# Weight conversions cast two steps behind their values, low parts on VectorE, and an opening in another order

## The chip, the cores and the metric

The kernel runs on one core of a Trainium2 chip. The metric is the device time of one launch in microseconds (us), the median of three runs. The core's engines work beside each other, each through its own queue in order: TensorE (PE: matmuls and transposes; weight loads are listed as PEld), VectorE (DVE), ScalarE (ACT), GpSimd (POOL) and SyncE (SP, which here only issues DMAs). Semaphores make one engine wait for another.

## What is computed

The reference chains three layers for 4 sequences of 576 tokens with 512 channels:

```python
attn = softmax(mask128(q @ k.T / 8 - slope * distance))      # 8 heads of 64, window of 128
x    = (attn @ v) laid out as tokens x 512
u    = x + real(fft(fft(x, axis=1), axis=2))                 # mixing
un   = (u - mean) / sqrt(var + 1e-6)
x2   = u + relu(un @ w_ch1) @ w_ch2                          # 2048 hidden; w_ch1, w_ch2 are float64
e    = argmax(x2 @ w_gate), or the expert of the token before it (local gate)
out  = p[e] * (relu(x2 @ w1[e]) @ w2[e])                     # 8 experts, 1024 hidden
```

## The kernel before

All large products run in fp32r as three matmuls on a high and a low part of each operand (`mm3`, L176 to L178); the high part is a cast (`split`, L172, ACT), the low part the rest after it (L173).

**Opening** (`opening`, written out by hand: inside `manual_schedule` the instructions of PE, DVE, ACT and POOL keep the program's order). Attention of sequence 0 runs over ten units; a unit is 128 query rows (or 65) for four heads. Its steps: `scores` on PE, bias and maximum on DVE (L395 to L398); `exps` on ACT (L405) with a small POOL addition (L406); `flip`: four PE transposes (L414), an ACT copy `w` (L418), POOL selects on `w` (L419, L421); `values` on PE (L433); `natural`: PE transposes back (L453) and a division on DVE (L461). Unit u's scores stand beside the flip of u-2, the values of u-3 and the natural of u-4. Then come the folds of x (L521 to L533), the first Fourier products `zps` (L950), their copies to SBUF (L988, `low_row` L581 and L582), the second products `pc` (L567), which `spread` adds to x (L559, L560), the statistics (L757), the normalised rows `u` (L791, L793), their transposes and the first MLP matmuls. POOL casts a small table `alt` (L859) that has come by DMA.

**Weights.** w_ch1 and w_ch2 arrive as 64-bit words in blocks of 128 x 512. Turning a block to fp32 takes a scaling on ACT (`early64`, L248, or L284) and a shift of the lower word (L250 on ACT for the first half of the weights, L285 on DVE for the second), then two DVE operations (`values32`, L286, L287), then `split`: cast on ACT, low part on POOL. A chunk of 256 hidden units has four blocks, two for its `t1` and two for its `t2`. In `load_weights64` both values of a pair come first, then both casts, then both low parts.

**Lanes.** After the opening a planner (`run`) interleaves generators by due times: MLP pieces, conversions, attention and mixing of the next sequence. `late_` and `behind` keep instructions behind others on their engine; Tile's own scheduler then settles the order on each engine. The MLP runs over nine groups of 256 tokens twice, first with 1024 hidden units (chunks A), then with the other 1024 (chunks B). Chunk 0 of A is converted in the opening, chunks 1 to 3 beside the first MLP group (`conversions`), chunks B later (`second`).

**Routing.** In the second MLP pass `finish_group` of the group before is stepped once per MLP piece: transposes, `route` (gate products, copy `lt` L1153, transposes `pn` L1157, softmax and argmax), then for some groups `assign` (scans over the tokens, `rows` L1219, `place` L1225). The experts follow.

Of the kernel before, what the change touches and what calls it, by code (L numbers as in the profile page):

```python
# [10 lines left out]
F32 = mybir.dt.float32  # L11
F32R = mybir.dt.float32r
# [41 lines left out]
MIX = ((25.1, 10), (51.1, 11), (77.1, 12), (102.1, 9))  # L54
CONV_ = (25, 9.5)
CONV2 = (8, 38)
# [108 lines left out]
def build(ctx, tc, a, out):  # L165
# [86 lines left out]

    def load_weights64(chunks, i, c, wp, words, early=None):
        q = CB // 2
        for _ in early or ():
            pass
        ms = []
        for j in range(2):
            ms.append(values32(raws[c][j], words, early is not None))
            if j == 0:  # L260
                yield
        t1 = wp.tile([P, 2, 4, CB], F32R, tag="w1", name="t1")
        for j in range(2):
            split(t1[:, 0, :, j * q:(j + 1) * q], t1[:, 1, :, j * q:(j + 1) * q], ms[j], nc.gpsimd)
        chunks[i] = (t1, None)
        yield
        ms = []
        for j in range(2):
            ms.append(values32(raws[c][2 + j], words, early is not None))
            if j == 0:  # L270
                yield
        t2 = wp.tile([P, 2, CB // P, DM], F32R, tag="w2", name="t2")
        for j in range(2):
            split(t2[:, 0, j].rearrange("p (k f) -> p k f", k=4), t2[:, 1, j].rearrange("p (k f) -> p k f", k=4), ms[j], nc.gpsimd)
        chunks[i] = (t1, t2)
        yield

    def values32(r, words, small=False):
# [4 lines left out]
        if not small:  # L283
            nc.scalar.activation(y.bitcast(F32), y.bitcast(F32), AF.Copy, scale=BIAS)  # L284
            nc.vector.tensor_single_scalar(wl, wl, 29, op=ALU.logical_shift_right)  # L285
# [79 lines left out]
    def attention(b, between=None):  # L365

        xs = xss[b] = [slab([P, 2, DM], F32, "x", "x", XB) for _ in range(3)]
        units = [(g, i) for g in range(2) for i in range(5)]
        copy = nc.vector.tensor_copy if b == 0 else nc.scalar.copy
# [98 lines left out]
        for u in range(len(units) + VL + 1):  # L468
            if ahead < 4 and u in (0, 2, 5):
                g, p = parts[ahead]  # L470
                R[g, p] = load_part(b, g, p)
                ahead += 1
            if u < len(units):
                scores(u)
            if 1 <= u < len(units) + 1:
                exps(u - 1)
            yield

            def fill():
                if b == 0 and u >= len(units) - 1:  # L480
                    spin(SPIN_)

            def back():
                if VL < u:
                    natural(u - VL - 1)

            def weights():
                if FL <= u < len(units) + FL:
                    flip(u - FL)
# [12 lines left out]
            yield  # L502
# [10 lines left out]
    def fold(xs, kt, eng=nc.vector, xf=None):  # L513
# [5 lines left out]
        if kt == 0:  # L519

            nc.vector.scalar_tensor_tensor(out=xe, in0=xb, scalar=inner[:, 0:1], in1=xa, op0=ALU.mult, op1=ALU.add)  # L521
        else:
            nc.vector.tensor_tensor(out=xe[0:m], in0=xa[0:m], in1=xb[0:m], op=ALU.add)
        if kt == 2:
            nc.scalar.copy(xe[32:33], xa[32:33])
        nc.vector.tensor_tensor(out=xe[0:n, 1:HN], in0=xe[0:n, 1:HN], in1=xe[0:n, DM - 1:HN:-1], op=ALU.add)
# [219 lines left out]
    def normalise(gs, xT, j, src=None):  # L746
# [106 lines left out]
    def tables():  # L853

        with tc.issue_after(last["load"].ins):
            alt32 = slab([P, KE], F32, "alt32", "m", MB)
            for t, x in ((alt32, "alt"), (tab1, "tab1"), (tab2, "tab2")):
                nc.sync.dma_start(out=t, in_=a[x])
        nc.gpsimd.tensor_copy(alt, alt32)  # L859

# [11 lines left out]
    def conversions():  # L872
        def places():
            for i in range(2 * (FA // CB - 1)):
                if i % 3:
# [3 lines left out]
                else:  # L879
                    yield sm.tile([P, 2 * CB], U32, tag="t64", name="t64", bufs=2)  # L880
                    yield sm.tile([P, 2 * CB], U32, tag="t64", name="t64", bufs=2)

        place = places()
        for c in range(1, FA // CB):
            yield from load_weights64(chunksA, c, c, wpA, lambda: next(place), soon64[c])

# [37 lines left out]
    def opening():  # L924
# [56 lines left out]

        idle[0] = ps_g.tile([P, DM], F32, tag="g", name="idle")
        bank.update({(1, 0): a2[:, 1], (1, 1): ps_h1.tile([P, DM], F32, tag="h", name="zps")})
        Z = [slab([P, 2, K1], F32, f"z{cs}", "m", MB) for cs in range(2)]
# [19 lines left out]
        def value():  # L1004
            ms.append(values32(raws[0][len(ms)], lambda: next(place), True))

# [17 lines left out]
        nrm = prepare(0, (xs[0][:, 0], xs[1][:, 0]))  # L1024
        words.step(4)
        for _ in range(3):
            next(nrm)
        next(nrm)
        value()
# [21 lines left out]
    def late_(it):  # L1051

        while True:
# [4 lines left out]
            if r is END:  # L1058
                return
            yield r  # L1060

    lanes = [lane(SETUP, 8, 1, setup()), lane(CONV_[0], CONV_[1], 4 * (FA // CB - 1), late_(conv)),
             lane(MLP_[0], MLP_[1], 4 * FA // CB * 9, mlp_first())]
# [18 lines left out]
    def second():  # L1082

        words = lact.tile([P, 4, 2 * CB], U32, tag="xTe", name="t64", bufs=1)
        turns = iter(range(4 * nB))
        for c in range(nB):
            it = load_weights64(chunksB, c, nA + c, wpB, lambda: words[:, next(turns) % 4])
            while True:
                with behind():
                    if next(it, END) is END:  # L1090
                        break
                yield

# [7 lines left out]
    now = min(x[0] for x in lanes)  # L1101
    lanes.append(lane(now + CONV2[0], CONV2[1], 4 * nB, second()))
    run(lanes)
# [38 lines left out]

    def route(gs, xT, apart):
        n = len(gs) * P
# [50 lines left out]
    def assign(b, half=None):  # L1195
# [26 lines left out]
        def place(g, st_, m):  # L1222
# [12 lines left out]
            if b == B - 1 and g in TAIL:  # L1235
                for x in placed:
                    tc.declare_no_dep(w.ins, x, reason="each token has a slot of its own")
                placed.append(w.ins)

        ready = None  # L1240
        for t in ts:
# [223 lines left out]
    def finish_group(gs, x2s, j):  # L1465
# [5 lines left out]
        if apart:  # L1471
            yield
        yield from route(gs, x2T, apart)
        if j in after:
# [193 lines left out]
```

## Time and profile before

| | us |
|---|---|
| median of three runs | 934.81 (934.53 to 934.94) |
| the profiled execution | 935.08 |
| its span | 933.4 |
| PE busy | 886.8 |
| DVE busy | 520.9 |
| ACT busy | 378.8 |
| POOL busy | 251.4 |

Busy time is the union of an engine's instructions. The views differ: the slices (windows) give busy time and granted clock of a stretch; the waits give an engine's idle time with what ended it; the timeline gives single instructions, with the idle time ahead of one in brackets and the releaser behind the arrow.

### The profile page before, as it was taken

Reading aid. Unit: us, or ns where it says so; the run is one execution under the profiler, and the core shown is the slowest. Engines: PE = TensorE matmul, PEld = TensorE weight load, DVE = VectorE, ACT = ScalarE, POOL = GpSimd, SP = SyncE. Lnnn points to the kernel's source line nnn. Section 1 sums busy time; section 2 is a strip of 40 time slices with the busy share of each in tenths; the row PEclk is TensorE's granted clock in tenths of the full one; section 3 lists DMA queues with packets and bytes.
Section 4 is the critical chain, followed back from the end, with each engine's and each line's share of the span. In section 5 each row is a group of like instructions: output and inputs, shape, how many; then the busy total and the mean of one; then the engine's idle time right before and its main releaser. Section 6 shows DMA issues by size and latency. Waiting matters only on the chain.

```text
span 933.4 us, 16250 instructions
## 1 busy us (share of the span) xinstructions
PE 886.8 (95%) x5954; PEld 747.2 (80%) x5958; DVE 520.9 (56%) x1326; ACT 378.8 (41%) x1003; POOL 251.4 (27%) x374
## 2 busy tenths in 40 slices
PE   8986899999999998999999999999999999999993
PEld 4665677777787897899888888887888898888882
DVE  4879957746746577521333635456874665556410
ACT  4684563653553245421121111113544554445410
POOL 2425731350322046210111222223331221032100
PEclk8998999999999999999999999999999999999997
DMA  9933251451403593263444252545635765555100
GB/s 321 333 124 103 84 188 59 145 161 44 137 25 102 158 359 111 68 158 69 113 113 104 51 117 70 114 113 189 188 118 183 239 221 172 173 181 177 68 21 20
DMA packets 103361, 128.20 MB, mean 137 GB/s; under 512 B 10577, under 2 KB 72401, under 8 KB 103239
## 3 DMA queue, kind: packets, MB, share of 16 engines
q1 hardware_dynamic: 77958, 102.98, 33.7%
q0 software_dynamic: 22720, 19.36, 9.5%
q10 hardware_dynamic: 2592, 4.72, 1.4%
q8 instruction: 49, 0.80, 0.4%
q14 instruction: 42, 0.34, 0.1%
HBM read 98.68 MB, written 30.19 MB: 138 GB/s over the span
## 4 chain that ended last, share of the span: by engine, by line
PE 70%; DVE 14%; issue 6%; ACT 3%; DMA 3%; POOL 2%; SPq 0%; DVEq 0%; POOLq 0%; ACTq 0%
PE hps L176 9%; PE acc L176 9%; PE hps L178 9%; PE hps L177 9%; PE acc L177 8%; PE acc L178 8%; PE s L393 3%; PE o L433 3%; DVE t L286 3%; PE tps L641 2%; PE zps L615 2%; DVE t L287 2%; PE acc L688 2%; PE pt L414 1%; PE xps L453 1%
## 5 line engine op out<-in xcount | busy, mean ns | idle before, releaser
L669 ACT ACTIVATE h<-hps 128x256 fp32r<-128x256 f32 x152 | 58.2, 383 | 264.5 <-PE hps L178 264.1
L672 DVE SCALAR_TENSOR_TENSOR h<-hps,h 128x256 fp32r<-128x256 f32 x152 | 63.8, 420 | 150.3 <-ACT h L669 149.5
L176 PE MATMUL acc<-t,h 128*128 128x512 f32 x312 | 129.2, 414 | 2.7 <-ACT t L172 2.5
L177 PE MATMUL acc<-t,h 128*128 128x512 f32 x312 | 124.1, 398 | 1.7 <-POOL t L173 1.7
L178 PE MATMUL acc<-t,h 128*128 128x512 f32 x312 | 123.4, 396 | 0.2 <-DVE h L672 0.2
L173 DVE TENSOR_TENSOR t<-we,t 128x512 fp32r<-128x512 f32 x128 | 85.9, 698 | 35.1 <-ACT t L172 34.4
L172 ACT CAST t<-we 128x512 fp32r<-128x512 f32 x128 | 74.6, 618 | 29.7 <-PE acc L688 17.2
L176 PE MATMUL hps<-xT,t 128*128 128x256 f32 x288 | 84.5, 294 | 1.4 <-DVE h L672 1.3
L176 PE MATMUL hps<-xTb,t 128*128 128x256 f32 x288 | 84.1, 292 | 0.0
L176 PE MATMUL hps<-xTe,t 128*128 128x256 f32 (+6 forms) x288 | 83.5, 290 | 0.0
L177 PE MATMUL hps<-xTe,t 128*128 128x256 f32 (+6 forms) x288 | 83.0, 288 | 0.0
L177 PE MATMUL hps<-xT,t 128*128 128x256 f32 x288 | 82.3, 286 | 0.6 <-DVE xT L173 0.6
L178 PE MATMUL hps<-xTe,t 128*128 128x256 f32 (+6 forms) x288 | 82.9, 288 | 0.0
L178 PE MATMUL hps<-xT,t 128*128 128x256 f32 x288 | 82.2, 286 | 0.6 <-POOL t L173 0.6
L178 PE MATMUL hps<-xTb,t 128*128 128x256 f32 x288 | 81.5, 283 | 0.0
L177 PE MATMUL hps<-xTb,t 128*128 128x256 f32 x288 | 81.5, 283 | 0.0
L405 ACT ACTIVATE t<-t,mx 128x128 f32<-128x128 f32 (+1 forms) x160 | 62.6, 393 | 40.6 <-DVE mx L398 35.5
L178 PEld LDWEIGHTS acc<-t,h 128*128 128x128 f32 x312 | 58.6, 188 | 15.0 <-DVE h L672 1.2
L176 PEld LDWEIGHTS acc<-t,h 128*128 128x128 f32 x312 | 58.9, 189 | 14.7 <-issue 3.1
L177 PEld LDWEIGHTS acc<-t,h 128*128 128x128 f32 x312 | 59.1, 189 | 9.6 <-POOL t L173 2.3
L672 DVE SCALAR_TENSOR_TENSOR hE<-hps,hE 128x256 fp32r<-128x256 f32 (+3 forms) x96 | 29.7, 338 | 60.5 <-ACT hE L669 60.2
L176 PEld LDWEIGHTS hps<-xT,t 128*128 128x128 f32 x288 | 55.1, 192 | 7.8 <-DVE h L672 1.9
(311 smaller groups left out, 2047.2 us busy)
## 6 DMA issues: line engine op xcount, KB each, us to landing
we<-in_w SPq DMA_DIRECT2D x64, 512.0 KB, 4.4
rw<-in_w_ch SPq DMA_DIRECT2D x32, 512.0 KB, 8.9
qkt<-in_qk SPq DMA_DIRECT2D x15, 642.0 KB, 4.2
nd<-xT SPq DMA_DIRECT2D x18, 512.0 KB, 3.7
xTb<-nd POOLq DMA_DIRECT2D x18, 512.0 KB, 6.0
vt<-in_v SPq DMA_DIRECT2D x16, 384.0 KB, 10.4
pd<-y ACTq DMA_DIRECT2D x18, 256.0 KB, 3.2
ub<-ud SPq DMA_DIRECT2D x18, 256.0 KB, 2.8
```

What stands on the lines that cost most here:

```text
L172: last["hi"] = nc.scalar.copy(hi, src)
L173: return (eng or nc.vector).tensor_tensor(out=lo, in0=src, in1=hi.bitcast(F32), op=ALU.subtract)
L176: nc.tensor.matmul(o, lhsT=wh, rhs=xh, start=start, stop=False, **kw)
L177: nc.tensor.matmul(o, lhsT=wh, rhs=xl, start=False, stop=False, **kw)
L178: return nc.tensor.matmul(o, lhsT=wl, rhs=xh, start=False, stop=stop, **kw)
L286: nc.vector.scalar_tensor_tensor(out=t, in0=y, scalar=3, in1=wl, op0=ALU.logical_shift_left, op1=ALU.bitwise_or)
L287: nc.vector.scalar_tensor_tensor(out=t, in0=y, scalar=0x80000000, in1=t, op0=ALU.bitwise_and, op1=ALU.bitwise_or)
L393: nc.tensor.matmul(o[h], lhsT=qt[r, x, q0:q0 + m], rhs=qt[r, x, k0:k0 + n0 + n1], start=i > 0, stop=True)
L405: nc.scalar.activation(t[0:m, j], t[0:m, j], AF.Exp, bias=mx[0:m, j:j + 1], scale=-1.0, accum_out=sums[0:m, j:j + 1])
L433: nc.tensor.matmul(o[h * D:(h + 1) * D, x, 0:m], lhsT=v[:, OWN[i] - z, (2 * x + h) * D:(2 * x + h + 1) * D], rhs=w[:, z, 2 * h + x, 0:m], ...
L669: last["relu"] = nc.scalar.activation(h[:, 0:n], hps[:, 0:n], AF.Relu)
L672: last["rest"] = nc.vector.scalar_tensor_tensor(out=h[:, lo:lo + c1 - c0], in0=hps[:, c0:c1], scalar=0.0, in1=h[:, c0:c1].bitcast(F32), op ...
```

## The change

1. Conversions (`convert` takes the place of `load_weights64`) go block by block. Step b makes the values of block b, the cast and the low part of block b-2, and the scaling of block b+1. The low part is a DVE subtraction (it was POOL's). For 12 blocks there are 14 steps (12 before) in a lane of 11 units (9.5 before); for chunks B there are 18 steps (16) in the same 38 units. What is left of `early64` is issued two instructions per block, behind the last MLP instructions.
2. The opening: `flip(0)` of sequence 0 comes ahead of `exps(1)`; the cast of `alt` comes nine steps later; the third fold no longer copies one row on ACT, since POOL zeroes that row of x at the start of each attention; the products of `zps` lie in other PSUM tiles; the statistics of the first half come ahead of the second half's products.
3. Three routing steps are set apart by one MLP piece each: `pn` of the eighth group, and the first `rows` of `assign` for sequences 0 and 1.

```diff
-CONV_ = (25, 9.5)
+CONV_ = (25, 11)
...
+    def convert(chunks, wp, cs, base, words, early=None):
+        blocks = [(c, h, j) for c in cs for h in range(2) for j in range(2)]
+        n, q = len(blocks), CB // 2
+        ts, made = {}, {}
+
+        def lift(b):
+            c, h, j = blocks[b]
+            if early is None:
+                lifted(raws[base + c][2 * h + j])
+                return
+            with behind() if "ffn" in last else nullcontext():
+                for _ in range(2):
+                    next(early[c], None)
+
+        lift(0)
+        for b in range(n + 2):
+            if b >= 2:
+                c, h, j = blocks[b - 2]
+                if j == 0:
+                    made[h] = wp.tile([P, 2, 4, CB] if h == 0 else [P, 2, CB // P, DM], F32R, tag=f"w{h + 1}", name=f"t{h + 1}")
...
+                t = ts.pop(b - 2)
+                nc.scalar.copy(hi, t)
+            if b < n:
+                ts[b] = values32(raws[base + blocks[b][0]][2 * blocks[b][1] + blocks[b][2]], words)
+            if b >= 2:
+                nc.vector.tensor_tensor(out=lo, in0=t, in1=hi.bitcast(F32), op=ALU.subtract)
+                if j == 1:
+                    chunks[c] = (made[0], made[1] if h else None)
+            if b + 1 < n:
+                lift(b + 1)
+            yield
...
     def attention(b, between=None):
 
         xs = xss[b] = [slab([P, 2, DM], F32, "x", "x", XB) for _ in range(3)]
+        nc.gpsimd.memset(xs[2][32:33, 1], 0.0)
...
+            if b == 0 and u == FL:
+                flip(0)
             if 1 <= u < len(units) + 1:
                 exps(u - 1)
...
-            nc.vector.tensor_tensor(out=xe[0:m], in0=xa[0:m], in1=xb[0:m], op=ALU.add)
-        if kt == 2:
-            nc.scalar.copy(xe[32:33], xa[32:33])
+            nc.vector.tensor_tensor(out=xe[0:n], in0=xa[0:n], in1=xb[0:n], op=ALU.add)
...
             nc.vector.bn_stats(st[:, i], src[i])
+            if i + 1 < n and not later:
+                yield
...
-                tables()
+                alt32 = tables()
+            if n == 13:
+                nc.gpsimd.tensor_copy(alt, alt32)
...
-                a2 = ps_a.tile([P, 2, DM], F32, tag="acc", name="zps")
-                bank.update({(0, 0): s2[:, 1], (0, 1): a2[:, 0], (0, 2): s2[:, 0]})
+                bank.update({(0, 0): s2[:, 1], (0, 1): ps_h1.tile([P, DM], F32, tag="h", name="zps"), (0, 2): s2[:, 0]})
...
-        bank.update({(1, 0): a2[:, 1], (1, 1): ps_h1.tile([P, DM], F32, tag="h", name="zps")})
+        a2 = ps_a.tile([P, 2, DM], F32, tag="acc", name="zps")
+        bank.update({(1, 0): a2[:, 0], (1, 1): a2[:, 1]})
...
         next(kb0)
+        nrm = prepare(0, (xs[0][:, 0], xs[1][:, 0]))
+        next(nrm)
+        next(nrm)
...
         nc.scalar.copy(lt[:, 0:n], ps[0:r2, 0:n])
         yield
+        if late_copy:
+            yield
...
+        if half is None and b < 2:
+            yield
         ready = None
         for t in ts:
             new = rows(t)
```

## Rows read from the trace of the kernel before

**Rows 1.** The page: engines over the span, and two-input subtractions on VectorE.

```profile
PE 886.8 (95%) x5954; PEld 747.2 (80%) x5958; DVE 520.9 (56%) x1326; ACT 378.8 (41%) x1003; POOL 251.4 (27%) x374
...
L173 DVE TENSOR_TENSOR t<-we,t 128x512 fp32r<-128x512 f32 x128 | 85.9, 698 | 35.1 <-ACT t L172 34.4
```

**Rows 2.** Windows: length, then busy of PE, PEld, DVE, ACT, POOL; clock, DMA, GB/s.

```profile
0.00:25.00 25.00, 21.12 (x132) 12.25 (x132) 11.81 (x23) 10.95 (x45) 5.11 (x17) 0.86 0.87 309
...
50.00:75.00 25.00, 21.53 (x131) 15.92 (x132) 20.23 (x45) 19.32 (x40) 7.35 (x7) 1.00 0.30 104
75.00:100.00 25.00, 18.79 (x119) 13.91 (x117) 25.00 (x37) 12.16 (x40) 15.52 (x14) 0.86 0.17 53
100.00:125.00 25.00, 20.38 (x166) 15.50 (x165) 19.53 (x37) 13.95 (x51) 16.42 (x29) 1.00 0.52 154
125.00:150.00 25.00, 24.98 (x213) 20.02 (x212) 10.66 (x27) 11.83 (x42) 6.52 (x13) 1.00 0.40 128
...
350.00:375.00 25.00, 21.94 (x138) 19.24 (x138) 20.19 (x32) 14.29 (x29) 16.41 (x20) 1.00 0.33 103
```

**Rows 3.** Waits of PE in the span: us in total, times, longest.

```profile
PE tp L1225 <- DVE sq L1219: 2.3, 4, 0.8
...
PE tps L641 <- ACT u L805: 2.2, 1, 2.2
...
PE o L433 <- POOL w L419: 2.0, 1, 2.0
...
PE pn L1157 <- ACT lt L1153: 1.3, 1, 1.3
```

**Rows 4.** Timeline of POOL, 15 to 16: start, us, what, [idle before <-releaser].

```profile
15.23 0.29 POOL L859 CAST alt<-alt 128x130 fp32r<-128x130 f32 x1 [1.14 <-DMA alt<-in_alt]
15.48 0.65 POOL L419 TENSOR_SCALAR_AFFINE_SELECT w<-w 128x512 f32<-128x512 f32 x1
```

**Rows 5.** Timeline of PE, 12 to 19.

```profile
12.04 1.13 PE L393 MATMUL s<-qkt 64*128 64x256 f32 x8
...
16.18 0.71 PE L433 MATMUL o<-w,vt 128*64 128x128 f32 x8 [2.02 <-POOL w L419]
16.82 2.08 PE L393 MATMUL s<-qkt 64*128 64x256 f32 x8
```

**Rows 6.** Timeline of ACT, the first copy w.

```profile
13.69 0.56 ACT L418 COPY w<-pt 128x512 f32<-128x512 f32 x1
```

**Rows 7.** Windows: the stretch behind the first wait, columns as in rows 2.

```profile
20.00:22.00 2.00, 2.00 (x18) 1.59 (x18) 1.73 (x5) 1.11 (x5) 0.90 (x2) 0.50 1.06 411
```

**Rows 8.** Timeline of DVE, 44 to 62.

```profile
44.00 0.48 DVE L526 TENSOR_TENSOR xf<-xf 33x255 f32<-33x255 f32 x1 [0.99 <-ACT xf L525]
...
61.20 0.42 DVE L559 TENSOR_TENSOR x<-x,pc 128x256 f32<-128x256 f32 x1 [1.37 <-PE pc L570]
...
61.87 1.28 DVE L757 BATCH_NORM_STATS2 st<-x 128x6 f32<-128x512 f32 x2
```

**Rows 9.** Timeline of PE, the last zps products.

```profile
55.95 1.24 PE L950 MATMUL zps<-tab,xf 128*128 128x289 f32 x4 [0.79 <-ACT z L988]
```

**Rows 10.** Groups by form, DVE, 72 to 114: count, busy us, mean ns, idle.

```profile
L286 DVE SCALAR_TENSOR_TENSOR t<-rw 128x512 uint32<-128x512 uint32 x11 | 12.1, 1117 | 0.0
L287 DVE SCALAR_TENSOR_TENSOR t<-rw,t 128x512 uint32<-128x512 uint32 x12 | 9.7, 830 | 0.0
```

**Rows 11.** Timeline of DVE: two L286 without POOL beside them, two with it.

```profile
88.86 1.27 DVE L286 SCALAR_TENSOR_TENSOR t<-rw 128x512 uint32<-128x512 uint32 x2
...
94.33 2.99 DVE L286 SCALAR_TENSOR_TENSOR t<-rw 128x512 uint32<-128x512 uint32 x2
```

**Rows 12.** Groups by form, POOL, 76 to 114.

```profile
L173 POOL TENSOR_TENSOR t<-t,t 128x512 fp32r<-128x512 f32 x12 | 17.6, 1485 | 9.7 <-ACT t L172 9.7
```

**Rows 13.** Timeline of ACT, 350: the casts of a pair.

```profile
350.47 1.14 ACT L172 CAST t<-t 128x512 fp32r<-128x512 f32 x2 [2.37 <-DVE t L287]
```

**Rows 14.** Timeline of PE, 352.

```profile
352.38 0.66 PE L641 MATMUL tps<-ident,u 128*128 128x128 f32 x4 [2.23 <-ACT u L805]
```

More of the change, by code (lines that the diff above doesn't have):

```diff
@@ L251, in early64 @@
             yield
[L253 to L276, printed above, removed]
@@ L278, in values32 @@
-    def values32(r, words, small=False):
+    def convert(chunks, wp, cs, base, words, early=None):
[16 more added lines that the diff above has]
+                    made[h] = wp.tile([P, 2, 4, CB] if h == 0 else [P, 2, CB // P, DM], F32R, tag=f"w{h + 1}", name=f"t{h + 1}")
+                if h == 0:
+                    hi, lo = (made[0][:, i, :, j * q:(j + 1) * q] for i in range(2))
+                else:
+                    hi, lo = (made[1][:, i, j].rearrange("p (k f) -> p k f", k=4) for i in range(2))
+                t = ts.pop(b - 2)
[9 more added lines that the diff above has]
+            yield
@@ L280, in values32, with lifted @@
+    def lifted(r):
+        w = r.rearrange("p k (n t) -> p k n t", t=2)
+        wl, y = w[:, :, :, 0], w[:, :, :, 1]
+        nc.scalar.activation(y.bitcast(F32), y.bitcast(F32), AF.Copy, scale=BIAS)
+        nc.vector.tensor_single_scalar(wl, wl, 29, op=ALU.logical_shift_right)
+    def values32(r, words):
         w = r.rearrange("p k (n t) -> p k n t", t=2)
@@ L282, in values32 @@
         t = words().rearrange("p (k n) -> p k n", k=4)
-        if not small:
-            nc.scalar.activation(y.bitcast(F32), y.bitcast(F32), AF.Copy, scale=BIAS)
-            nc.vector.tensor_single_scalar(wl, wl, 29, op=ALU.logical_shift_right)
         nc.vector.scalar_tensor_tensor(out=t, in0=y, scalar=3, in1=wl, op0=ALU.logical_shift_left, op1=ALU.bitwise_or)
@@ L488, in weights @@
                 if FL <= u < len(units) + FL:
-                    flip(u - FL)
+                    if b or u > FL:
+                        flip(u - FL)
                     fill()
@@ L858, in tables @@
                 nc.sync.dma_start(out=t, in_=a[x])
-        nc.gpsimd.tensor_copy(alt, alt32)
+        return alt32
     def setup():
@@ L873, in places @@
         def places():
-            for i in range(2 * (FA // CB - 1)):
-                if i % 3:
+            while True:
+                for _ in range(2):
+                    yield sm.tile([P, 2 * CB], U32, tag="t64", name="t64", bufs=2)
+                for _ in range(2):
                     t = wraw.tile([P, 4 * CB], U32, tag="r64", name="t64", bufs=RB)
@@ L878, in places @@
                     yield t[:, 2 * CB:]
-                else:
-                    yield sm.tile([P, 2 * CB], U32, tag="t64", name="t64", bufs=2)
-                    yield sm.tile([P, 2 * CB], U32, tag="t64", name="t64", bufs=2)
         place = places()
-        for c in range(1, FA // CB):
-            yield from load_weights64(chunksA, c, c, wpA, lambda: next(place), soon64[c])
+        yield from convert(chunksA, wpA, range(1, FA // CB), 0, lambda: next(place), soon64)
     END = object()
@@ L974, in opening @@
                 s2 = ps_s.tile([P, 4, 2 * P], F32, tag="s", name="zps").rearrange("p (a b) c -> p a (b c)", a=2)
-                a2 = ps_a.tile([P, 2, DM], F32, tag="acc", name="zps")
-                bank.update({(0, 0): s2[:, 1], (0, 1): a2[:, 0], (0, 2): s2[:, 0]})
+                bank.update({(0, 0): s2[:, 1], (0, 1): ps_h1.tile([P, DM], F32, tag="h", name="zps"), (0, 2): s2[:, 0]})
+                idle[0] = ps_g.tile([P, DM], F32, tag="g", name="idle")
                 zprod(2, (0,))
@@ L980, in opening @@
         folding(1)
-        idle[0] = ps_g.tile([P, DM], F32, tag="g", name="idle")
-        bank.update({(1, 0): a2[:, 1], (1, 1): ps_h1.tile([P, DM], F32, tag="h", name="zps")})
+        a2 = ps_a.tile([P, 2, DM], F32, tag="acc", name="zps")
+        bank.update({(1, 0): a2[:, 0], (1, 1): a2[:, 1]})
         Z = [slab([P, 2, K1], F32, f"z{cs}", "m", MB) for cs in range(2)]
@@ L1004, in value @@
         def value():
-            ms.append(values32(raws[0][len(ms)], lambda: next(place), True))
+            ms.append(values32(raws[0][len(ms)], lambda: next(place)))
         copies(0)
@@ L1023, in opening @@
         spin(FILL)
-        nrm = prepare(0, (xs[0][:, 0], xs[1][:, 0]))
         words.step(4)
@@ L1027, in opening @@
             next(nrm)
-        next(nrm)
         value()
@@ L1060, in late_ @@
             yield r
-    lanes = [lane(SETUP, 8, 1, setup()), lane(CONV_[0], CONV_[1], 4 * (FA // CB - 1), late_(conv)),
+    lanes = [lane(SETUP, 8, 1, setup()), lane(CONV_[0], CONV_[1], 4 * (FA // CB - 1) + 2, late_(conv)),
              lane(MLP_[0], MLP_[1], 4 * FA // CB * 9, mlp_first())]
@@ L1085, in second @@
         turns = iter(range(4 * nB))
[L1086 to L1092, printed above, removed]
+        it = convert(chunksB, wpB, range(nB), nA, lambda: words[:, next(turns) % 4])
+        while True:
+            with behind():
+                if next(it, END) is END:
+                    return
+            yield
     spare = lact.tile([P, 4, DM], F32, tag="x2T", name="spare", bufs=1)
@@ L1101, in build @@
     now = min(x[0] for x in lanes)
-    lanes.append(lane(now + CONV2[0], CONV2[1], 4 * nB, second()))
+    lanes.append(lane(now + CONV2[0], CONV2[1], 4 * nB + 2, second()))
     run(lanes)
@@ L1141, in cols, with route @@
         return ap[:, :, s0:(e if e >= 0 else None):-1]
-    def route(gs, xT, apart):
+    def route(gs, xT, apart, late_copy):
         n = len(gs) * P
@@ L1238, in place @@
                 placed.append(w.ins)
+        if half is None and b < 2:
+            yield
         ready = None
@@ L1472, in finish_group @@
             yield
-        yield from route(gs, x2T, apart)
+        yield from route(gs, x2T, apart, j == 7)
         if j in after:
```

## The prediction

> **What bounds the kernel now.** I read the busy times first, then the windows, the waits of PE, and last the timelines around each wait. PE is busy 886.8 of 933.4 us [rows 1]: the end is set by PE's work plus the time in which it has none, 46.6 us. The windows show where that is [rows 2]. From 125 on PE is full (24.98 of 25), and VectorE has slack (10.66). Ahead of that, PE lacks 3.9 us in the first 25, and 14.3 us from 50 to 125 (3.5 + 6.2 + 4.6), where VectorE is the full engine: 25.00 of 25 from 75 to 100. A smaller hole of 3.1 us lies at 350 to 375. The waits name what ended the holes [rows 3]: a select on POOL once (2.0), a normalisation on ACT once (2.2), routing copies on VectorE (2.3 in four) and the copy `lt` (1.3). So a part of the change is worth what it takes from PE's path in the opening, from VectorE's queue in 57 to 114, and from single waits later. Behind 125 a shift stays whole, since PE is full there and no row shows it waiting for a transfer.
>
> **The change part by part.** Sums are made against the profiled execution: 933.4 us of span and 1.7 around it are 935.08; the median of the runs shown is 0.27 lower.
>
> *The first select.* PE waits 2.02 us for `w` [rows 5]. POOL had the cast of `alt` in front of the select; it waited for its DMA until 15.23, and the select ran at 15.48 for 0.65 [rows 4]. ACT made its copy at 13.69, behind the exponentials of unit 1 [rows 6]. The cast now comes later, and the copy goes ahead of those exponentials. The transposes that it reads were done when the next scores began, at 12.04 [rows 5]. So: copy 12.1 to 12.7, select to 13.4. The exponentials of unit 1 start 0.5 later, so the transposes that PE does ahead of `values` end near 14.6, and PE goes on at 14.6 in place of 16.18: -1.6. Then the clock. The same eight scores took 1.13 us ahead of the wait and 2.08 behind it [rows 5], and the granted clock of 20 to 22 is 0.50, which is the 1.2 GHz level [rows 7]; PE had stood still for 2.02 us before it fell. Without that pause PE should keep the 2.4 GHz level. From 16.8 to about 23, six microseconds of work at half the clock would take three; VectorE and ACT, one unit apart, allow some of that. Bounds 0 and -3.0, taken -2.4. Sum -4.0 (range -1.6 to -4.6). The cast of `alt` is wanted 40 us later and costs nothing; POOL's new zeroing of one row stands at its start, where it is idle (5.11 of 25 busy).
>
> *The third fold.* VectorE stands 0.99 us for the ACT copy of one row [rows 8]. It goes; the same addition takes 33 rows in place of 32, which costs nothing, as time goes by columns. The products behind it follow VectorE: -1.0 (range -0.4, if PE's transposes of the ninth unit are late next, to -1.0).
>
> *PSUM tiles and statistics.* The last four `zps` wait 0.79 us for an ACT copy [rows 9] that reads the other half of the tile they write. With both halves of that tile belonging to them the wait goes: -0.8 (0 to -0.8). Then VectorE stands 1.37 us for the second `pc` and does two statistics behind it, 1.28 for both [rows 8]. The first of them now fills that gap: -0.6. It is queued ahead of the second half's additions, which wait for PE anyway.
>
> *Conversions of chunks 1 to 3.* Added on VectorE: 12 low parts at 0.67 (85.9 us for 128 of the same form [rows 1]): +8.0. Removed: the slowing of VectorE by POOL's subtractions. Two L286 take 1.27 with POOL quiet and 2.99 with a subtraction beside them [rows 11]. Over the stretch the 11 and 12 value operations took 21.8 us [rows 10]; at 0.64 each they would take 14.7: 7.1 lost. The opening's own pair, which stays on POOL, and the selects have a part in that, while the additions of `spread` lose something too that is not counted: returned 6.5. The lane is 1.5 units longer, so work of attention and MLP that stood behind the conversions now stands among them. At 125 to 150 such work costs VectorE 10.66 while PE does 24.98 [rows 2]: of each microsecond so moved 0.57 is won. Estimate: 1.5 of 11 units of a stretch of 42 us, at PE's pace some 2.5 us, -1.5. Sum 0. A low part waits for a cast that is issued ahead of two value operations; queued behind it are the bias and maximum of the next scores, for which PE waits. No row shows that wait: bounds 0 and 0.6 each (a quarter of the 2.37 that ACT spends on values in rows 13), together +7.1. Other end: each of the 12 subtractions had blocked VectorE for its whole time, 17.6 us [rows 12]: 8.0 - 17.6 - 1.5 = -11.1. So +7 to -11, taken 0, by the rows of the value operations themselves.
>
> The Trainium skill ("SBUF — State Buffer", "Who interferes with whom") says that a VectorE instruction with two SBUF inputs and a GpSimd instruction that reads SBUF exclude each other for a whole instruction. The 2.99 against 1.27 agree with it. Taken at its word it also speaks against the change: the low part is a third such instruction per block, open to POOL's selects; by rows that would take back part of the 6.5, by the rule up to all of it.
>
> *Conversions of chunks B.* ACT stood 2.37 us on the values for a pair of casts [rows 13], the normalisation came behind, and PE waited 2.23 for it [rows 14]. With casts two steps behind, ACT finds its input ready: -2.2. VectorE gets 16 low parts, +10.7, in a stretch where it has 20.19 of 25 [rows 2] with POOL's slowing in it. PE is the full engine there; what may come late next is the low half of the hidden values: +0.4. Sum -1.8 (range -3.0 to +2).
>
> *Routing.* `pn` gets a piece more: -1.3, if the copy is done by then. Two of the four waits for `rows` are set apart; at 0.6 each of 2.3 in four [rows 3], -1.2. I take -2.4 (0 to -2.5). The steps behind them have room in a group of 32 pieces.
>
> Sum: -4.0 - 1.0 - 0.8 - 0.6 + 0 - 1.8 - 2.4 = -10.6: 924.5 for a profiled execution, 924.2 for the median.
>
> **Rivals.**
> 1. *The opening gives it back.* PE loses the POOL wait, but the next unit waits for VectorE or ACT, the clock falls to 0.50 all the same, and the select's part is worth only its first bound, -1.6, with the fold at -0.4: 927.2. For it: PE follows exponentials one by one there. Against: only one PE wait of that length is listed.
> 2. *VectorE gets all back.* Each POOL subtraction had cost VectorE most of its 17.6 us. At two thirds, 11.7, the conversions end at 8.0 - 11.7 - 1.5 = -5.2: 919. This is what the exclusion rule of the Trainium skill named above would make of it. For it: VectorE at 25.00 of 25. Against: the value operations show 7.1.
> 3. *The change of order does not do what it says.* The scheduler settles the order outside the opening by itself. The waits at 352 and in routing come back under other names: 924.2 + 4.2 = 928.4.
> 4. *Slower: VectorE's line.* In 57 to 114 each low part waits for a cast behind exponentials, 12 times 0.6, and the selects take all that is returned: +8.0 + 7.1 - 1.5 = +13.6; in chunks B the same makes +1 of -1.8. Sum -6.4 + 13.6 + 1.0 - 2.4 = +5.8: 941. It decides from the point at which the first conversions cost 10.6. Against: ACT is half idle there (12.16 of 25).
>
> **How the numbers follow.** Forecast 924.2: 0.60, with its own range 920.5 to 928. Rival 1: 0.13; 2: 0.12; 3: 0.08; 4: 0.07. The range 917 to 932 holds the forecast and rivals 1 to 3 and leaves out the fourth and the far end of the second. A measurement of this kernel tells 0.2% (1.9 us) from no change. Faster by more: 0.89 (forecast, 1, 2 and most of 3); within: 0.04 (edges of 1 and 3); slower: 0.07 (rival 4).
>
> **What would show it.** In the profile after: no PE wait for the select and a clock of 1.00 from 16 to 24; the first MLP matmuls 5 to 7 us earlier; L286 and L287 near 0.65 us between 60 and 105 with POOL's subtractions gone and low parts on VectorE; PE full from a point 5 to 8 us earlier than 125; no PE wait for a normalisation in chunks B; no wait for `lt`. Wrong would be: VectorE idle ahead of its low parts behind ACT casts, PE full no earlier than before, or a half clock in the opening.

## The result, and the profile after

The changed kernel takes 924.85 us (median of four runs, 922.24 to 925.8) where the kernel before took 934.88 beside it: ratio 0.9887, 95% interval 0.9865 to 0.991. The forecast was 924.2. Measured again on another chip (e5, below) it takes 924.61 beside 933.01: ratio 0.991, which is 8.4 us. The profiled execution of the first measurement took 924.03, its span is 922.3.

The windows of the changed kernel that answer to those of before [rows 2] (columns: stretch and its length, busy us and count of PE, PEld, DVE, ACT and POOL, granted clock, DMA share, GB/s):

```profile
0.00:25.00 25.00, 21.86 (x174) 13.12 (x174) 16.12 (x35) 14.82 (x61) 8.40 (x23) 1.00 0.92 327
50.00:75.00 25.00, 21.54 (x142) 16.18 (x142) 22.06 (x46) 14.14 (x37) 7.89 (x6) 1.00 0.31 101
75.00:100.00 25.00, 20.56 (x146) 14.99 (x145) 24.96 (x46) 18.25 (x53) 11.28 (x11) 0.93 0.20 59
100.00:125.00 25.00, 20.97 (x156) 15.51 (x155) 14.91 (x37) 14.36 (x51) 8.45 (x23) 0.97 0.54 178
125.00:150.00 25.00, 24.91 (x202) 20.30 (x202) 12.55 (x34) 8.66 (x34) 5.35 (x10) 0.96 0.25 82
350.00:375.00 25.00, 24.20 (x156) 21.71 (x155) 21.53 (x42) 14.10 (x28) 8.12 (x10) 1.00 0.23 76
```

In the first 25 us the granted clock is 1.00 where it was 0.86, and the hole at 350 to 375 is filled: PE is busy 24.20 of 25, where it had 21.94. But from 100 to 125 PE still stands 4.0 us, and now VectorE is not the full engine there (14.91). Something else holds it. PE's waits name candidates (columns: us in total, times, longest; some of the list):

```profile
PE pt L430 <- DVE x L477: 1.7, 1, 1.7
...
PE acc L178 <- DVE h L689: 1.5, 2, 0.8
PE tp L1246 <- DVE sq L1240: 1.4, 2, 0.8
...
PE tps L658 <- ACT u L824: 1.2, 1, 1.2
```

Of the waits of before [rows 3], the select's 2.0, the normalisation's 2.2 in chunks B and the copy `lt`'s 1.3 are gone; the routing rows have 1.4 in two for 2.3 in four. New are `pt` (1.7) and `tps` (1.2), both between 100 and 125. The wait of `acc` for the low half of the hidden values (`h`), which was 0.2 before, is 1.5 in chunks B.

The opening, by the timeline of POOL, ACT and PE (start, us, engine, line, operation, idle time before in brackets):

```profile
11.79 0.65 POOL L435 TENSOR_SCALAR_AFFINE_SELECT w<-w 128x512 f32<-128x512 f32 x1 [0.74 <-ACT w L434]
...
11.13 0.58 ACT L434 COPY w<-pt 128x512 f32<-128x512 f32 x1 [0.42 <-PE pt L430]
...
13.57 0.66 PE L449 MATMUL o<-w,vt 128*64 128x128 f32 x8
14.16 1.13 PE L409 MATMUL s<-qkt 64*128 64x256 f32 x8
```

PE comes to the values with no wait, and the eight scores behind them take 1.13, not 2.08 [rows 5]. The granted clock from 16 to 24 is 1.00.

The new hole: SyncE's and VectorE's timelines around the loads of the second group's rows.

```profile
101.48 0.33 SPq L760 DMA_DIRECT2D r<-ud  x1
102.26 0.33 SPq L884 DMA_DIRECT2D ent<-in_ent  x1
102.66 0.65 SPq L885 DMA_DIRECT2D slots<-in_empty  x1
103.36 0.57 SPq L888 DMA_DIRECT2D x2d<-in_zero  x1
104.06 0.50 SPq L760 DMA_DIRECT2D r<-ud  x1
...
104.86 0.69 DVE L774 BATCH_NORM_STATS2 st<-r 128x6 f32<-128x512 f32 x1 [0.58 <-DMA r<-ud]
109.89 0.69 DVE L774 BATCH_NORM_STATS2 st<-r 128x6 f32<-128x512 f32 x1 [3.01 <-DMA r<-ud]
```

Three setup transfers, about 1.4 MB by their shapes, are issued between the two row loads `r`. The first row load is used 3.4 us after its issue, the second 5.8 after, and VectorE stands 3.01 in front of it with the maximum of the next scores queued behind. In the kernel before, both row loads were issued ahead of the setup: the second at 113.45, used at 116.24, 2.8 later. No line of the diff touches the setup; its due time is 45 in both. The conversions' part alone brings the new order: e2, below, has the setup between the row loads (105.65 and 108.23), e1 has both loads ahead of it. And with the low parts back on GpSimd, steps and due times as changed, both loads are ahead again (e8: 102.23 and 106.27, the setup from 106.65). So the due times alone don't make this order; Tile's scheduler, which settles it on each engine, has a part.

To compare stages I take four marks from the traces: the start of the last of the 16 matmuls with which PE begins (`warm`), PE's first MLP matmul, and the starts of the two ACT copies of MLP output near 250 and near 430 that the timeline shows as a pair (x2). The first two columns are times from the span's start, the others the lengths of the stages behind them, in single profiled executions:

| | last warm | first MLP | to ~250 | to ~430 | to the end |
|---|---|---|---|---|---|
| before | 7.0 | 68.9 | 187.4 | 174.2 | 502.8 |
| changed | 5.8 | 61.8 | 189.0 | 171.3 | 500.1 |
| changed again (e5) | 7.2 | 63.0 | 187.5 | 171.4 | 500.1 |
| opening alone (e1) | 7.3 | 63.6 | 186.3 | 174.0 | 502.7 |
| conversions alone (e2) | 6.1 | 66.2 | 187.0 | 172.5 | 502.0 |
| routing alone (e3) | 6.7 | 68.9 | 187.4 | 174.1 | 500.8 |
| setup later (e4) | 7.1 | 62.9 | 184.1 | 171.4 | 502.6 |
| low parts on POOL (e8) | 6.2 | 62.0 | 188.0 | 179.8 | 499.9 |
| lane of 9.5, setup later (e11) | 7.2 | 63.0 | 186.8 | 171.8 | 502.1 |
| lane of 12.5, setup later (e12) | 5.9 | 61.7 | 187.3 | 171.6 | 500.2 |

The warm matmuls are the same work in all of them; the last one's start moves by 1.5 us from one execution to the next, so times of the first MLP matmul are compared less that. Stages vary too: the two executions of the changed kernel differ by 1.5 to ~250, and in the longer one the granted clock from 100 to 150 is 0.97 and 0.96, in the other 1.00.

### The profile page after: what moved, and what is told of

Same layout as the page of the kernel before. It is cut to its first block, busy times and chain, and to the rows that moved or that the text cites. A ratio compares the mean times of both kernels' runs of the same rounds, so it can differ in the third digit from the quotient of the medians.

```text
span 922.3 us, 16219 instructions
## 1 busy us (share of the span) xinstructions
PE 882.5 (96%) x5954; PEld 746.1 (81%) x5958; DVE 518.3 (56%) x1354; ACT 376.4 (41%) x999; POOL 228.1 (25%) x350
## 4 chain that ended last, share of the span: by engine, by line
PE 72%; DVE 11%; issue 6%; DMA 4%; ACT 4%; POOL 3%; SPq 0%; POOLq 0%; DVEq 0%; ACTq 0%
PE hps L176 10%; PE hps L177 10%; PE hps L178 10%; PE acc L176 9%; PE acc L177 9%; PE acc L178 9%; PE s L409 2%; PE o L449 2%; PE tps L658 2%; PE zps L632 2%; PE acc L705 2%; ACT t L421 1%; DMA r<-ud 1%; DVE t L282 1%; PE pt L430 1%
## 5 line engine op out<-in xcount | busy, mean ns | idle before, releaser
L178 PEld LDWEIGHTS acc<-t,h 128*128 128x128 f32 x312 | 58.7, 188 | 16.1 <-DVE h L689 2.7
```

Source lines behind the costliest of these rows:

```text
L178: return nc.tensor.matmul(o, lhsT=wl, rhs=xh, start=False, stop=stop, **kw)
```

## The experiments

The theory: the prediction's mechanisms hold, and the setup transfers between the row loads give back about 3 us that the conversions won. The rivals are the prediction's own and those in the expectations.

**The three parts alone (e1, e2, e3).** Each is the kernel before with one part of the diff:

```diff
e1  +            if b == 0 and u == FL:
    +                flip(0)                 # with: cast of alt late, third fold, PSUM tiles, statistics
e2  -    def load_weights64(...)
    +    def convert(...)                    # with: lane 11, places, values32, 14 and 18 steps
e3  +        if late_copy:
    +            yield
    +        if half is None and b < 2:
    +            yield
```

> The kernel before with the opening's edits alone (first select ahead of the exponentials, cast of alt later, third fold without its row copy, PSUM tiles, statistics). The prediction's terms for these sum to -7.0 (-4.0 -1.0 -0.8 -0.6 = -6.4, and up to -0.6 for its rounding): 928.5, range 926.5 to 930; no PE wait for the select, granted clock 1.00 from 16 to 24, first MLP matmul some 6 us earlier. Rival (the opening gives it back): clock falls to 0.50 again and only -3.4 stays: 931.5. Second rival: what the opening gains is lost again between 60 and 125, where VectorE and not PE is full: first MLP matmul 6 us earlier, but the time only 1 to 3 us shorter: 932 to 934.

> The kernel before with the conversions' edits alone (single blocks, casts two steps behind, low parts on VectorE, lane of 11, tiles). The prediction has 0 for chunks 1 to 3 and -1.8 for chunks B: 933.1. New theory after the two traces: VectorE's line is about 6 us shorter there, and the three setup transfers that now stand between the two row loads give 3 to 4 of it back, so chunks 1 to 3 come out at -1 to -3 and the part at 930 to 932. Rival 2 (VectorE gets all back, -5.2 and -1.8): 928. Rival 4 (low parts wait for casts, selects take the rest): 941. To be seen: low parts of 0.67 each, two row loads with setup between them, the second landing 5 us or more after its issue.

> The kernel before with the three pieces set apart in routing alone. Prediction: no PE wait for the copy lt (-1.3) and two of four waits for rows gone (-1.2): -2.4, 932.5. Rival (the order is settled by the scheduler, or the waits come back under other names): 0 to -0.5, 934.4 to 934.9. The changed kernel still shows 1.4 us in two waits for rows against 2.3 in four, by which it would be -0.9 -1.3 = -2.2.

Measured beside a before of 933.11: e1 926.58, ratio 0.9933 (0.9916 to 0.995); e2 931.18, 0.9981 (0.9968 to 0.9993); e3 932.21, 0.9986 (0.9975 to 0.9997). The three savings add to 0.0100, some 9.3 us of 933; the whole change had 0.0113, and 0.0090 in e5. Within the intervals the parts add up. e1's 0.0067 is 6.3 us, for terms that sum to 6.4 (the 7.0 in its expectation is a slip). The opening keeps its gain to the end: counted from the last warm matmul, e1's first MLP matmul comes 5.6 us earlier, and the stages behind it are as before or shorter, which speaks against both of its rivals. The conversions come out at 1.8, as the prediction's two terms for them have it, and between its rivals 2 and 4. Routing comes out at 1.3 (0.3 to 2.3), short of the 2.4 expected.

**The setup transfers later (e4) and earlier (e6).**

```diff
-SETUP = 45
+SETUP = 55        # e6: 35
```

> The changed kernel with one number changed: the due time of the three setup transfers is 55 in place of 45, so that SyncE issues them behind both row loads and behind the next queries and values. New theory: the second row load lands some 3 us after its issue in place of 5.8, VectorE's 3.0 us in front of the second statistics goes, and PE's waits at 111.6 (1.7) and 116 (1.2) with it: 921 to 922 where the changed kernel has 924.9, a gain of 3 to 4. Rival: another load is late next, or the second row load waits for its buffer and not for the channel: no gain, 924 to 925.5. Second rival: the setup transfers now hold up the loads of queries and values that follow, and it is slower: 926.

> The changed kernel with the due time of the three setup transfers at 35 in place of 45: they are now issued ahead of both row loads, not between them. Theory (the second row load lands late because 1.4 MB are issued just ahead of it): they start as soon as SyncE has issued the values' load, some microseconds before 101, and are partly through; the wait of VectorE falls from 3.0 us to 0 to 1.5, and the time is 1 to 3 us below the changed kernel. Rival (the second row load waits for its buffer, which the conversions free late): the wait stays, no change within 1 us. Second rival: both row loads are late now: the same time or 1 to 3 us more.

e4: 922.79, ratio 0.9889 (0.9869 to 0.9909). The changed kernel once more (e5, on another chip), whose expectation was:

> The changed kernel once more, beside the others and on their chip, so that they have it to be compared with. Ratio to before as already measured, 0.989 (0.9865 to 0.991); by the sum of the three parts run alone (0.9933, 0.9981, 0.9986) it would be 0.990.

gave 924.61 and 0.991 (0.9894 to 0.9926); e6 gave 924.15 and 0.9915 (0.989 to 0.9939). e4's ratio lies 0.002 below e5's, with intervals that overlap: in the time it is a tendency only, and the 3 to 4 us expected of it are not there. Its trace is plain. SyncE, VectorE and the window of 100 to 125:

```profile
102.59 1.91 SPq L760 DMA_DIRECT2D r<-ud  x2
...
105.88 0.70 DVE L774 BATCH_NORM_STATS2 st<-r 128x6 f32<-128x512 f32 x1 [0.48 <-DMA r<-ud]
107.07 0.69 DVE L774 BATCH_NORM_STATS2 st<-r 128x6 f32<-128x512 f32 x1
...
100.00:125.00 25.00, 23.86 (x194) 18.01 (x194) 17.11 (x42) 16.47 (x59) 9.50 (x24) 1.00 0.45 143
```

The wait of 3.01 us ahead of the second statistics is gone, PE has 23.86 of 25 (20.97), and the waits for `pt` and `tps` are not listed in that stretch. The stage to ~250 is 3.4 us shorter than e5's. So the loss at this point is shown, and its cause, the order of issue: the buffer was not what the load waited for. Then the last stage, with the routing, takes 2.5 back (502.6 against 500.1). VectorE's timeline, first of e4, then of the changed kernel:

```profile
639.32 0.17 DVE L1437 CAST idn<-ids 128x4 uint32<-128x4 f32 x1 [2.20 <-DMA ids<-slots]
```

```profile
640.40 0.17 DVE L1437 CAST idn<-ids 128x4 uint32<-128x4 f32 x1 [0.44 <-DMA ids<-slots]
```

`ids` is read back from `slots` behind POOL's last scatter (an indexed DMA that writes `slots`). In e4 the last two scatters start at 623.69 and 631.04, in the changed kernel at 626.36 and 631.60: a lead of 2.7 us is down to 0.6. Why the last one starts so late in e4 was not tried; of the two other runs with the setup at 55, e11 has the longer last stage too (502.1) and e12 has not (500.2).

In e6 the theory missed: VectorE's wait was to fall to 0 to 1.5 and rose to 4.46, with the time as before, so its second rival holds. SyncE issues its transfers in order, and the setup, due earlier, still stood behind the load of values `vt`, which went out at 101.31; then both row loads were behind the setup.

```profile
101.31 0.33 SPq L334 DMA_DIRECT2D vt<-in_v  x1
...
102.86 0.58 SPq L888 DMA_DIRECT2D x2d<-in_zero  x1
103.99 0.82 SPq L760 DMA_DIRECT2D r<-ud  x2
...
110.40 1.37 DVE L774 BATCH_NORM_STATS2 st<-r 128x6 f32<-128x512 f32 x2 [4.46 <-DMA r<-ud]
```

The Trainium skill ("DMA: Bandwidth & Descriptors", "Two DMAs through the same engine are not ordered") says that within one queue of a DMA engine descriptors start in order, though an earlier one need not have finished writing when a later one completes. The traces agree: the row load issued behind 1.4 MB from the same queue was used 5.8 us after its issue, the one ahead of it 3.4, the second one of before, with no setup ahead, 2.8.

**The first select undone (e7), and its two edits one by one (e9, e10).**

```diff
e7, e9   -            if b == 0 and u == FL:
         -                flip(0)
         -                    if b or u > FL:
         -                        flip(u - FL)
         +                    flip(u - FL)
e7, e10  -                alt32 = tables()
         -            if n == 13:
         -                nc.gpsimd.tensor_copy(alt, alt32)
         +                nc.gpsimd.tensor_copy(alt, tables())
```

> The changed kernel with the opening's first select as it was (copy behind the exponentials of unit 1, cast of alt ahead of the select). By the prediction's term: PE waits some 2 us for the select again, the clock falls to 0.50 for a stretch behind it, and the time is 4.0 us longer (1.6 the wait, 2.4 the clock). Rival 1: the wait alone counts, 1.6. Second rival: PE's gain at 16 us is lost ahead of the MLP where VectorE or ACT decides, 0 to 0.5.

> The changed kernel with only the copy of the first select back behind the exponentials of unit 1 (the cast of alt stays late). The prediction took both edits together; POOL is free when the copy is done, so the select should end some 0.7 us behind the copy at about 13.7, 14.4, and PE wait about 0.5 to 1 us: 0.5 to 1.5 longer than the changed kernel, the clock at 1.00. Rival (the wait is as before, since the copy and not the cast of alt had decided): 3 to 4 longer, the clock at 0.50 behind it.

> The changed kernel with only the cast of alt back where it was, in POOL's line ahead of the second or third select, the copy early. By the prediction the cast waits for its transfer until about 15.2 us and every select queued behind it with it. Since the first select now stands ahead of the cast or behind it according to where its copy was put, either it waits as before (3 to 4 longer, clock 0.50) or only the next select waits, whose values PE needs later (0 to 1 longer).

e7: 928.04, ratio 0.9942 (0.9921 to 0.9963), 3.4 us above e5, which ran on the same chip, near the 4.0 expected (the intervals of the two ratios just touch). e9: 924.42, 0.9908 (0.9884 to 0.9933). e10: 925.16, 0.9911 (0.9886 to 0.9936). With one edit undone, whichever, nothing is lost that can be measured; with both, 3.4. PE's timelines of e9 and e10, and POOL's of e10:

```profile
14.90 0.66 PE L449 MATMUL o<-w,vt 128*64 128x128 f32 x8 [0.86 <-POOL w L435]
```

```profile
13.99 0.66 PE L449 MATMUL o<-w,vt 128*64 128x128 f32 x8
...
12.21 0.65 POOL L435 TENSOR_SCALAR_AFFINE_SELECT w<-w 128x512 f32<-128x512 f32 x1 [0.74 <-ACT w L434]
...
14.33 0.29 POOL L971 CAST alt<-alt 128x130 fp32r<-128x130 f32 x1 [0.33 <-DMA alt<-in_alt]
```

With the copy early the select goes ahead of the cast; with the cast late the select goes at once behind its late copy. Only where the copy was late *and* the cast stood in front did both meet.

The clock is another matter. Here is PE in two executions with the select as before, first e3, then e7, each with a window behind it (columns as above; the granted clock is the third number from the end):

```profile
16.40 1.12 PE L433 MATMUL o<-w,vt 128*64 128x128 f32 x8 [2.58 <-POOL w L419]
17.45 2.08 PE L393 MATMUL s<-qkt 64*128 64x256 f32 x8
...
18.00:20.00 2.00, 2.00 (x11) 1.22 (x8) 0.42 (x1) 0.00 (x0) 0.28 (x2) 0.50 1.10 354
```

```profile
16.36 0.66 PE L449 MATMUL o<-w,vt 128*64 128x128 f32 x8 [2.50 <-POOL w L435]
16.95 1.14 PE L409 MATMUL s<-qkt 64*128 64x256 f32 x8
...
18.00:20.00 2.00, 2.00 (x28) 1.64 (x28) 1.73 (x3) 0.38 (x1) 0.98 (x4) 1.00 1.12 363
```

Nearly the same pause, 2.58 and 2.50 us, and behind it the clock is at the 1.2 GHz level (0.50) in one execution and at 2.4 (1.00) in the other. e2's profile also has the wait (2.92) and keeps 1.00. e7's six runs fall into two groups: 924.4 and 925.1 with a mean granted clock of 0.992 and 0.990, and 928.0 to 929.9 with 0.984 to 0.987; those of e5 lie at 923.8 to 925.6 (0.988 to 0.992). In the ten profiles without this pause the clock stays at 1.00 from 4 to 50. So in these traces the fall at this place comes only behind the pause, but not always, and by e7's two groups it is the fall, where it comes, that costs.

**Low parts on GpSimd (e8).**

```diff
-                nc.vector.tensor_tensor(out=lo, in0=t, in1=hi.bitcast(F32), op=ALU.subtract)
+                nc.gpsimd.tensor_tensor(out=lo, in0=t, in1=hi.bitcast(F32), op=ALU.subtract)
```

> The changed kernel with the 28 low parts back on GpSimd, blocks and order otherwise as changed. With it SyncE's order falls back by itself: both row loads stand ahead of the setup transfers, so it is to be compared with the run in which these are due at 55 (ratio 0.9889 to before) as well as with the changed kernel. By the prediction, VectorE's 8.0 us of low parts in the first conversions and 10.7 in the second cost as much as GpSimd's contention did (6.5 and the rest): within 1.5 us of that run. Rival 2 (each subtraction on GpSimd costs VectorE most of its length): 3 to 6 us slower. Rival 4 (VectorE's low parts were the burden): 3 to 6 us faster. To be seen: value operations of 0.64 beside VectorE's low parts, and how long they take beside GpSimd's.

930.42, ratio 0.9975 (0.9961 to 0.9988): 5.8 above e5 on the same chip, and 0.0086 (8.0 us) above e4, to which its setup order answers. The expected "within 1.5 us" was wrong; it is rival 2's direction and beyond its 3 to 6, the largest single effect found. VectorE by groups from the opening's end through the first conversions, first the changed kernel (66 to 104), then e8 (66 to 106); columns: busy us, mean ns of one, idle before:

```profile
L301 DVE SCALAR_TENSOR_TENSOR t<-rw 128x512 uint32<-128x512 uint32 x11 | 8.5, 775 | 0.0
L282 DVE TENSOR_TENSOR t<-t,t 128x512 fp32r<-128x512 f32 x12 | 8.4, 703 | 0.0
L302 DVE SCALAR_TENSOR_TENSOR t<-rw,t 128x512 uint32<-128x512 uint32 x11 | 7.6, 690 | 0.0
...
L577 DVE TENSOR_TENSOR x<-x,cmb 128x256 f32<-128x256 f32 (+2 forms) x4 | 2.7, 685 | 0.0
...
L576 DVE TENSOR_TENSOR x<-x,cmb 128x256 f32<-128x256 f32 (+2 forms) x3 | 1.2, 405 | 0.0
```

```profile
L301 DVE SCALAR_TENSOR_TENSOR t<-rw 128x512 uint32<-128x512 uint32 x11 | 9.3, 861 | 0.0
L302 DVE SCALAR_TENSOR_TENSOR t<-rw,t 128x512 uint32<-128x512 uint32 x11 | 9.2, 852 | 0.0
L577 DVE TENSOR_TENSOR x<-x,cmb 128x256 f32<-128x256 f32 (+2 forms) x4 | 4.9, 1234 | 0.0
...
L576 DVE TENSOR_TENSOR x<-x,cmb 128x256 f32<-128x256 f32 (+2 forms) x4 | 3.2, 799 | 0.0
```

The values and the additions of `spread` together take 20.0 us beside VectorE's own low parts and 26.6 beside GpSimd's, with one addition more (0.4): some 6.2 us of contention against 8.4 us of low parts, nearly even, as forecast. The stage to ~250 is 3.9 longer than e4's all the same: PE waits there for two of GpSimd's selects, 2.23 us at 97.8 and 0.54 at 99.0, which stood behind two low parts in GpSimd's queue (93.77 to 96.7). e4 has no such wait. The larger loss is in chunks B, 8.4 us (179.8 against 171.4). Around 355 to 361, VectorE, GpSimd and PE of e8:

```profile
355.51 1.77 DVE L301 SCALAR_TENSOR_TENSOR t<-rw 128x512 uint32<-128x512 uint32 x1 [1.19 <-POOL t L282]
357.20 1.50 DVE L294 TENSOR_SCALAR rw<-rw 128x512 uint32<-128x512 uint32 x1
358.62 1.75 DVE L302 SCALAR_TENSOR_TENSOR t<-rw,t 128x512 uint32<-128x512 uint32 x1
360.29 0.74 DVE L689 SCALAR_TENSOR_TENSOR h<-hps,h 128x256 fp32r<-128x256 f32 x2
...
353.73 6.08 POOL L282 TENSOR_TENSOR t<-t,t 128x512 fp32r<-128x512 f32 x4
...
360.75 0.79 PE L178 MATMUL acc<-t,h 128*128 128x512 f32 x1 [3.17 <-DVE h L689]
```

GpSimd had the next group's normalisation first (twelve small operations from 347.98 to 353.7), so four low parts ran in a row behind it. VectorE first waits for one of them (1.19), then its three operations take 1.77, 1.50 and 1.75 where they take 0.68, 0.41 and 0.68 alone (361 to 362.6, the next block). The low half of the hidden values stands behind them, and PE waits 3.17 for it. With 2.92 at 344 these waits are 6.1 us in chunks B, where the changed kernel has 1.5, and behind the second the granted clock is 0.50 from 360 to 364. This is a queue that blocks a queue. The Trainium skill ("SBUF — State Buffer", "Who interferes with whom") also counts single-input operations that can run in a mode with two ports among those that a GpSimd instruction blocks; the `L294` of 1.50 beside it, 0.41 alone, agrees.

e8 also says that the conversions' two edits belong together. The opening's and routing's savings alone (e1, e3) add to 0.0081 with the old conversions; e8, with the same opening and routing and the new order of blocks, keeps 0.0025. As far as the parts add up, the new order with GpSimd's low parts costs some 5 us against the old one, and VectorE's low parts make up for it.

**The lane's length (e11, e12),** both with the setup at 55:

```diff
-CONV_ = (25, 11)
+CONV_ = (25, 9.5)      # e12: 12.5
```

> The changed kernel with the setup transfers due at 55, and the lane of the first conversions at 9.5 in place of 11. It is to be compared with the run in which the lane is 11 and the setup at 55 (ratio 0.9889 to before). The prediction gives the longer lane 1.5 us: here 1.5 longer, ratio 0.9905. Rival (the lane's length only moves the same work): within 0.5 us. Second rival: the shorter lane brings the MLP's first chunks earlier and is 1 us faster.

> The changed kernel with the setup transfers due at 55, and the lane of the first conversions at 12.5. If the prediction's estimate for the lane holds on, 1 to 1.5 us faster than the run with 11 (ratio 0.9875 to before, 921.4). Rival: the MLP's pieces now wait for their chunks, and it is 1 to 3 us slower.

e11: 925.5, ratio 0.991 (0.9885 to 0.9936); e12: 924.01, 0.9912 (0.9887 to 0.9937); e4 with 11 had 0.9889. Both lie 0.002 above, inside the intervals. To ~250 e11 takes 186.8 and e12 187.3, e4 184.1; in e12 one wait of `tps` for the normalisation on ACT is 3.9 us. But e12 has the shorter last stage, and by the spans of the profiles (923.8 and 920.8, e4 921.0) it is level with e4. So 11 is the best of three for that stage, which is the direction of the prediction's 1.5 us, and the times do not separate them. No run here is shown to beat the changed kernel; e4 is the candidate.

## Why the prediction was right, step by step

The total (-10.6 forecast; -10.0 measured in medians, -8.4 in e5) is right because most terms were, and by luck, because two errors of opposite sign met in the conversions.

- *First select, -4.0.* Measured 3.4 (e7 against e5). The mechanism was right: counted from the last warm matmul PE comes to the values 1.4 us earlier (1.6 forecast). Its split was not. It gave 1.6 to the wait and 2.4 to the clock as if the clock fell each time. The runs of e7 with a high clock lie within the changed kernel's; those with a low one are 3.4 to 5.3 above 924.61. How much the wait alone costs is not settled: e7's first MLP matmul comes 2.6 us later than e5's, counted from the last warm matmul, and by the end 2.3 are left, in a single profile with a high clock.
- *Fold, PSUM tiles, statistics, -2.4.* VectorE's third fold runs through with no ACT copy in it, the wait of `zps` for an ACT copy is gone (one of 0.88 for a fold on POOL is left, 1.02 before), and one statistic runs in the gap that `pc` leaves (53.37, gap 0.64 for 1.37). No run took them singly; e1's 6.3 (0.0067 of 933) less 3.4 leaves 2.9 for the three.
- *Conversions, chunks 1 to 3, 0.* The stage to ~250 is as long as before (187.5 in e5 for 187.4). The terms: low parts 8.4 (forecast 8.0), values 16.1 in 22 where 23 took 21.8 [rows 10], so some 5 returned (6.5), and no low part waits for its cast (VectorE's idle time before `L282` is 0.0). Two terms were missing. The additions of `spread` lose to GpSimd's low parts too: eight took 8.1 in the kernel before (72 to 114) and in e8, seven take 3.9 in the changed kernel, so 3.8 more are returned; the prediction named that and did not count it. And the row loads: the sum has VectorE's work alone and puts a new order of SyncE's transfers at nothing, without a row; that is the step that failed, and in the stage to ~250 it costs 3.4 (e5 against e4). That these two nearly cancel is luck. The lane's -1.5 rests on "some 2.5 us" that don't follow from its own figures (1.5 of 11 units of 42 us are 5.7); e11 and e12 do not settle it.
- *"Behind 125 a shift stays whole".* It holds for the opening's gain (e1) and fails in e4, where 2.5 of 3.4 are lost again behind ~430, at a DMA that VectorE waits for.
- *Conversions, chunks B, -1.8.* The stage from ~250 to ~430 is 2.9 shorter in the changed kernel, 1.7 in e2; the `tps` wait [rows 14] is gone. The low half of the hidden values came late as feared: PE waits 1.5 for it in two (0.2 before), against +0.4 forecast.
- *Routing, -2.4.* The last stage is 2.7 shorter (2.0 in e3); e3's time says 1.3, interval 0.3 to 2.3, so the 2.4 was somewhat too much.
- *The signs.* Most came: no wait for the select, a clock of 1.00, the first MLP matmul 5.9 us earlier counted from the last warm one, no wait for `lt`. One that was to mean "wrong" came too: PE is full no earlier than before. From 100 to 125 it has 20.97 (20.38 before), and its last wait of that stretch ends at 122.7 where it was 117.7. With the stage to ~250 as long as before, what stands at 250 is the opening's gain and nothing of the first conversions; chunks B and routing add theirs behind.
- *Rivals.* 1 (the opening gives it back) fails: clock 1.00, e1's gain whole. 2 (VectorE gets back 11.7) had the right cause and too much of it in the first conversions: 8.8 came back against the kernel before (5.0 and 3.8), 6.2 by e8, and with the row loads in order (e4) the stage to ~250 is 3.3 shorter than before, between the forecast's 0 and its 5.2. 3 fails: of the waits named only the one for `rows` came back, 1.4 in two. 4 fails: low parts never waited for a cast in the first conversions, and 0.5 in all in chunks B.

## What to carry to other kernels

Where a planner and a scheduler settle the order, a change in one lane can move DMAs of others on the same issuing queue: read the order of that queue around the change before and after, and keep bulk transfers that nobody waits for behind small loads that someone does. Where two engines can do the same work, ask what stands ahead of it and behind it in each one's queue: the low parts on GpSimd cost most through what queued behind them. Where two causes meet in one wait, removing either may be enough, so try them singly before keeping both.

## What the runs showed of the hardware that was not expected

After a pause of PE of 2 to 3 us the granted clock fell to 0.50 in some executions (2.02 in the kernel before, 2.58 in e3) and stayed at 1.00 in others (2.50 in e7, 2.92 in e2), with the same instruction order up to there. The two in which it fell had started their last warm matmul later (7.0 and 6.7 against 6.1 and 6.2); four executions don't show that this decides it. In one execution of e8 it stayed behind a pause of 2.92 and fell behind one of 3.17.

The last of the 16 warm matmuls starts between 5.8 and 7.3 us in executions of the same code, a start that varies by as much as an edit is worth. A single one takes 0.38 to 0.63 us, and more of them are long where the last starts late (the median is 0.63 in the kernel before and 0.38 in the changed one). The granted clock reads 1.00 there in both, so the rows don't show why.

A lead of 3.3 us (e4 at the first scatter of the last group, 613.32 against 616.65) shrank to 1.1 at the gather (640.39 against 641.46), behind a transfer for which the changed kernel waits only 0.44.
